# Gated linear attention and FFN on one core: the later units' state and score products in quarter tiles, joined into one row

## The chip, the cores and the metric

The kernel runs on one core of a Trainium2 chip. The metric is the device time of one execution in microseconds, as the median of several runs. Inside the core, TensorE multiplies matrices, VectorE, ScalarE and GpSimd work elementwise on what it leaves in PSUM, and SyncE's queue moves data by DMA. In the profile they are PE, DVE, ACT, POOL and SP; PEld is TensorE's loading of weights.

## The reference

Eight heads of four sequences, 768 tokens each, go through a linear attention whose state decays by a gate for each key dimension. Their outputs, 3072 tokens of 384, go through a two-layer FFN. q, k, v and alpha are float32, w_in and w_out are float64.

```python
for t in range(S):                       # S = 768; B, H, D = 4, 8, 48
    state = alpha[:, :, t, :, None] * state + np.einsum('bhd,bhe->bhde', k[:, :, t], v[:, :, t])
    y[:, :, t] = np.einsum('bhd,bhde->bhe', q[:, :, t], state)
x = y.transpose(0, 2, 1, 3).reshape(3072, 384)
h = x @ w_in                             # 384 x 2048
g = np.maximum(0.01 * h, h)
out = (g @ w_out).astype(np.float32)     # 2048 x 384
```

## The kernel before

**Attention.** The tokens are cut into chunks of 128. A unit u is one chunk of one sequence with all eight heads; there are 24, in order of the chunk and then of the sequence. Heads go in four pairs p, one head of a pair on partitions 0 to 47 (s = 0), the other on 64 to 111 (s = 1). For each unit, `scans` forms running products of alpha on VectorE (pc forward, rc backward), `scaled_q` and `scaled_k` transpose q and k and multiply them by these, and `scores` (L356) multiplies k by q for each head into two PSUM banks, which `mask_scores` copies and masks to sm (one bank on ScalarE and GpSimd, the other on VectorE, L364). `k_tokens` (L380) transposes k back to tokens. `outputs` then adds state times q (L395, for a pair at once, a block-diagonal 112x112 state) and values times masked scores (L401, two heads side by side in the columns), forms the new state's k v products (L412), and splits y into a high and a low part, ScalarE rounding it (L418) and VectorE subtracting (L419). `next_state` adds the products to the state (L436) and scales it by the decay on GpSimd (L373). In words used below: S is the scores, P state times q, V the values, K the k v products, t the transposes.

**FFN.** Three units make a block of 384 tokens; there are eight blocks. For each of 16 slices of 128 hidden columns, `ffn_in` makes one input product I: nine matmuls (three row groups of x, each as high x high, high x low, low x high) into a bank named ph (L493). ScalarE scales by 0.01 (L496), VectorE takes the maximum (L499), and the result is again split into gh (L501) and gl (L505). Three slices later `ffn_out` makes one output product O: nine matmuls into the block's three banks (L520). `gather` moves the spare rows of x into their places by DMA when a block's third unit is done.

**Order.** Units 0 to 8 come first (the head). Then blocks 0 and 1 run through the FFN while VectorE and ScalarE turn the float64 weights into high and low parts. From block 2 on, units 9 to 23, the later units, are woven in between the FFN's products: a generator yields slices of a unit's work, eight a unit (`SL`, `LEAD`), and the main loop takes as many as are due before each half item. A scheduler then fixes each engine's order by dependences; `tc.issue_after` pins an instruction behind another. PSUM has eight banks. Two rotate under ph; of six others, three hold a block's outputs (b) and three serve the attention (a). Tiles are given banks and SBUF as they are asked for, so a tile waits for whoever used its place before.

## Time and profile before

| | |
|---|---|
| runs | 531.2, 531.43, 532.03 us, median 531.43 us |
| profiled execution, span of the core | 530.9 us (page; what lies around the span isn't recorded for it) |
| granted TensorE clock, mean | 0.994 |
| TensorE busy | 518.5 us, 98% |
| VectorE busy | 379.0 us, 71% |
| ScalarE busy | 230.7 us, 43% |
| GpSimd busy | 62.6 us, 12% |

The page's lines give for each engine its busy time, its share of the span and the number of instructions. TensorE's rows count records: one float32 product is two records, so the scores' 8 products of a unit are 16. A row of a timeline has the start, the time in which the group was busy, engine, line, operation, output tile, input tiles, the tile of the array as rows*columns, the moving data and the count. The end of a matmul is modelled, so the time that a group takes is read from its start to the start of the next. A windows row has the window, its length, the busy time and count of each engine, the granted clock and the DMA share.

### The profile page before, as it was taken

The numbers are of one execution on the slowest core, as the hardware profiler recorded it, in microseconds if no ns is written. First come the engines' busy times: TensorE is split into PE (matmuls) and PEld (weight loads), VectorE is DVE, ScalarE is ACT, GpSimd is POOL, SyncE is SP. The second block draws the span as 40 slices with busy tenths as digits, with TensorE's granted clock in tenths as the row PEclk, the third lists the DMA queues.
The fourth block names the chain that finished last, engine by engine and source line by source line (L and its number), as shares of the span: only waits on it lengthen the run. The fifth ranks groups of instructions, "written<-read, shape, count | busy, mean of one in ns | idle before, by whom it ended". The sixth has DMA issues, their size and how long they took to land.

```text
span 530.9 us, 9962 instructions
## 1 busy us (share of the span) xinstructions
PE 518.5 (98%) x3778; PEld 500.0 (94%) x3778; DVE 379.0 (71%) x695; ACT 230.7 (43%) x489; POOL 62.6 (12%) x143
## 2 busy tenths in 40 slices
PE   8997999999999999999999999999999999999995
PEld 7886999999999999999999999999999999999995
DVE  6998899999999997777577586585786534333331
ACT  2764855555534444444334444345344444333331
POOL 4554500000000111100101101101010000000000
PEclk9998999999999999999999999999999999999998
DMA  9999975545726533552251431433201000101001
GB/s 144 168 175 170 229 172 133 131 122 141 170 45 184 127 84 81 102 134 49 60 111 30 112 83 44 92 74 86 54 15 25 31 16 1 23 1 44 1 0 51
DMA packets 92982, 46.64 MB, mean 88 GB/s; under 512 B 57856, under 2 KB 90112, under 8 KB 92928
## 3 DMA queue, kind: packets, MB, share of 16 engines
q1 hardware_dynamic: 92928, 45.93, 39.5%
q8 instruction: 32, 0.52, 0.4%
q14 instruction: 22, 0.18, 0.1%
HBM read 38.83 MB, written 4.72 MB: 82 GB/s over the span
## 4 chain that ended last, share of the span: by engine, by line
PE 87%; DVE 7%; DMA 4%; issue 1%; SPq 0%; DVEq 0%; ACT 0%
PE ph L493 35%; PE b L520 32%; PE a L356 4%; PE a L401 3%; PE a L520 3%; DMA small<-in_v_dram 3%; PE a L395 3%; PE a L412 2%; PE b L401 1%; PE a L380 1%; PE b L280 1%; DMA small<-in_alpha_dram 1%; DVE pw L262 1%; DVE gl L505 1%; DVE t L499 1%
## 5 line engine op out<-in xcount | busy, mean ns | idle before, releaser
L493 PE MATMUL ph<-large,w 128*128 128x384 f32 x1152 | 226.6, 338 | 0.5 <-DVE t L499 0.5
L493 PEld LDWEIGHTS ph<-large,w 128*128 128x128 f32 x1152 | 200.1, 188 | 2.8 <-DVE t L499 1.1
L520 PE MATMUL b<-w,gh 128*128 128x384 f32 x672 | 168.9, 340 | 0.0
L499 DVE TENSOR_TENSOR t<-ph,t 128x384 f32<-128x384 f32 x128 | 70.7, 553 | 79.1 <-ACT t L496 78.9
L520 PEld LDWEIGHTS b<-w,gh 128*128 128x128 f32 x672 | 119.4, 188 | 2.1 <-issue 0.4
L496 ACT ACTIVATE t<-ph 128x384 f32<-128x384 f32 x128 | 62.5, 489 | 128.2 <-PE ph L493 128.2
L501 ACT CAST gh<-t 128x384 fp32r<-128x384 f32 x128 | 65.7, 513 | 119.6 <-DVE t L499 119.6
L520 PE MATMUL b<-w,gl 128*128 128x384 f32 x336 | 107.4, 335 | 0.0
L505 DVE TENSOR_TENSOR gl<-t,gh 128x384 fp32r<-128x384 f32 x128 | 70.9, 554 | 34.3 <-ACT gh L501 34.2
L520 PEld LDWEIGHTS b<-w,gl 128*128 128x128 f32 x336 | 62.6, 188 | 0.0
L367 POOL TENSOR_SCALAR_AFFINE_SELECT sm<-sm 128x512 f32<-128x512 f32 x33 | 23.1, 712 | 207.8 <-ACT sm L366 207.8
L356 PEld LDWEIGHTS a<-qs,ks 48*128 48x128 f32 x312 | 24.1, 188 | 5.1 <-issue 4.2
L356 PE MATMUL a<-qs,ks 48*128 48x128 f32 x312 | 28.7, 285 | 0.0
L289 DVE STREAM_TRANSPOSE ks<-small 128x512 f32<-128x512 f32 x15 | 16.7, 1123 | 14.6 <-PE a L380 14.6
L324 POOL COPY pe<-pc 128x4 f32<-128x4 f32 x24 | 4.8, 202 | 163.7 <-DVE pc L314 163.7
L373 POOL TENSOR_TENSOR small<-us,pe 48x192 f32<-48x192 f32 x40 | 22.4, 560 | 1.5
L314 DVE TENSOR_TENSOR_SCAN pc<-e,small 128x128 f32<-128x128 f32 x60 | 20.4, 401 | 0.0
L366 ACT COPY sm<-a 128x512 f32<-128x512 f32 x24 | 14.0, 583 | 14.0 <-PE b L356 12.9
L520 PE MATMUL a<-w,gh 128*128 128x384 f32 x96 | 19.6, 337 | 0.0
L320 DVE TENSOR_TENSOR_SCAN rc<-e,small 128x511 f32<-128x511 f32 x15 | 19.1, 1276 | 0.2
L401 PE MATMUL a<-sm,small 128*48 128x128 f32 x256 | 17.7, 277 | 0.0
L254 ACT CAST w<-bits 128x768 fp32r<-128x768 f32 x16 | 13.4, 838 | 8.4 <-DVE bits L251 7.8
(92 smaller groups left out, 554.4 us busy)
## 6 DMA issues: line engine op xcount, KB each, us to landing
raw<-in_moe_w_out_dram SPq DMA_DIRECT2D x16, 384.0 KB, 3.8
small<-in_v_dram SPq DMA_DIRECT2D x24, 192.0 KB, 3.7
raw<-in_moe_w_in_dram SPq DMA_DIRECT2D x32, 144.0 KB, 4.0
out_dram<-o SPq DMA_DIRECT2D x24, 192.0 KB, 2.0
small<-in_alpha_dram SPq DMA_DIRECT2D x32, 96.0 KB, 2.3
small<-in_q_dram SPq DMA_DIRECT2D x30, 96.0 KB, 2.4
small<-in_k_dram SPq DMA_DIRECT2D x30, 96.0 KB, 2.2
small<-in_alpha_dram SPq DMA_DIRECT2D x30, 80.0 KB, 2.4
```

The source lines that it names most:

```text
L314: nc.vector.tensor_tensor_scan(pc[:, p, :], aT[:, p, :], ones.broadcast_to([P, C]), 1.0, ALU.mult, ALU.mult)
L320: nc.vector.tensor_tensor_scan(flat[2][:, NP * C - 2::-1], flat[0][:, NP * C - 1:0:-1], flat[1][:, NP * C - 2::-1], last, ALU.mult, ALU.add)
L356: nc.tensor.matmul(ss[s][:, p, :], ks[lo:lo + D, p, :], qs[lo:lo + D, p, :], start=True, stop=True)
L367: made["mask", u] = nc.gpsimd.affine_select(out=sm[s], in_=sm[s], compare_op=ALU.is_ge, fill=0.0, base=0, pattern=[[0, NP], [1, C]], chann ...
L373: nc.gpsimd.tensor_tensor(*scalings.pop(0))
L401: nc.tensor.matmul(y[lo:lo + m, p, :], V[:, c:c + m], masked[u][s][:, p, :], start=not tb and p == 0, stop=p == NP - 1, skip_group_check=True,
L493: nc.tensor.matmul(ph, w_in_of(f, wn, g), xt[:, g, :], start=n == 0, stop=n == 3 * NG - 1)
L496: put(ordered, "ACT", lambda: nc.scalar.mul(t, ph, 0.01))
L499: put(ordered, "DVE", lambda: nc.vector.tensor_tensor(t, ph, t, ALU.max))
L501: put(ordered, "ACT", lambda: nc.scalar.copy(gh, t))
L505: made["gl", i, f] = put(ordered, "DVE", lambda: nc.vector.tensor_tensor(gl, t, gh.bitcast(F32), ALU.subtract))
L520: product = nc.tensor.matmul(po[j], gt[:, js], w_out_of(f, wn), start=f == 0 and n == 0, stop=f == NF - 1 and n == 2)
```

## The change

**Scores.** For a later unit the 128 columns of weights are cut in two halves, M = HB = 64: 16 products, each on a quarter of the array (one half of the rows, one half of the columns), where there were 8 of half the array.

**State times q.** Four products of 112x112 become eight, one for each head, in the order that `heads` gives: q (0, 1), s (the head of the pair, the row half) and top (which pair, p = q + 2 top, the column half). A later unit uses 48 rows by 64 or 48 columns, a quarter; its two banks are one of the attention's, which also takes the k v products, and one of ph. An early unit uses 112 rows by 64 or 48 columns and one bank. `values` writes in the same places.

**One row.** `attention_later` replaces `attention` for units 9 to 23. It has seven slices a unit, and one of them issues past(u), scores(u+1), values(u) and products(u) with each instruction pinned behind the one before. I and O are pinned in the same line (`in_row`). The first scores wait until block 1's outputs are finished (`not (1 in pos and emitted == 3)`).

**x and tiles.** x now has heads 0 to 3 on the lower partitions and 4 to 7 on the upper; `runs`, which loads w_in's rows to match, changes in its first row and its strides, with as many DMAs of the same size. `split` copies a later unit's x in two halves, one for each bank. pe and us get fixed places (`ends_sb`, `sums_sb`), and pc and rc of later units one place each (`up`, `down`). The fallback `stepwise`, which these inputs do not reach, is adapted to the new places of x.

```diff
@@
     AHEAD = 3 * UPB
     LAG = 3
     SOON, EARLY = 2, 3
-    LEAD = 8
-    SL = 8 * UPB
+    LEAD = 7
+    SL = 7 * UPB
     kinds = ["a", "b"]
...
@@
-    runs = [(0, D, 0, 1, 2 * D), (D, GAP, 6 * D, NG, 1), (HB, D, D, 1, 2 * D), (BR, GAP, 7 * D, NG, 1)]
+    runs = [(0, D, 0, 1, D), (D, GAP, NG * D, NG, 1), (HB, D, NP * D, 1, D), (BR, GAP, (NP + NG) * D, NG, 1)]
     jobs = {}
@@
     def scans(u):
         aT = transposed(u, 0, "e", bufs=1)
-        pc = atp.tile([P, NP, C], F32, name="pc")
-        rc = atp.tile([P, NP, C], F32, name="rc")
-        pe = atp.tile([P, NP, 1], F32, name="pe", bufs=3)
+        pc, rc = (
+            atp.tile([P, NP, C], F32, name=name, bufs=2 if u < AHEAD else 1) for name in (("pc", "rc") if u < AHEAD else ("up", "down"))
+        )
+        pe = ends_sb[u % 3]
         for p in range(NP):
             nc.vector.tensor_tensor_scan(pc[:, p, :], aT[:, p, :], ones.broadcast_to([P, C]), 1.0, ALU.mult, ALU.mult)
         nc.vector.memset(every(aT, 0), 0.0)
@@
         pe, qs, ks = live[u]
         ss = [banks4(), banks4()]
+        M = C if u < AHEAD else HB
         for p in range(NP):
             for s, lo in ((0, 0), (1, HB)):
-                nc.tensor.matmul(ss[s][:, p, :], ks[lo:lo + D, p, :], qs[lo:lo + D, p, :], start=True, stop=True)
+                for t in range(0, C, M):
+                    yield ss[s][t:t + M, p, :], ks[lo:lo + D, p, t:t + M], qs[lo:lo + D, p, :], True, True
         live[u].append(ss)
     def mask_scores(u):
@@
             made["sm", u] = nc.scalar.copy(ktok.rearrange("t p d -> t (p d)"), kt[:, 0:NP * BR])
             live[u][2] = ktok
-    def outputs(u):
+    def heads():
+        for q in range(2):
+            for s, lo in ((0, 0), (1, HB)):
+                for top in range(2):
+                    yield q, s, lo, top, q + 2 * top, top * HB
+    ys = {}
+    def past(u):
         tb, b = units[u]
-        i, j = divmod(u, UPB)
+        qs, W = live[u][1], state[b].rearrange("r p n -> r (p n)")
+        if u < AHEAD:
+            y = banks4()
+            ys[u] = [y[:, s::2, :] for s in (0, 1)], y
+        else:
+            first = bank()
+            full = [first, ps_h.tile([P, 512], F32, name="ph")]
+            ys[u] = [t[:, 0:2 * C].rearrange("r (p n) -> r p n", p=2) for t in full], first[:, 2 * C:2 * C + NP * D]
+        if tb:
+            for q, s, lo, top, p, at in heads():
+                r = slice(0, BR) if u < AHEAD else slice(lo, lo + D)
+                c, m = p * BR + lo, D if top else HB
+                yield ys[u][0][s][at:at + m, q, :], W[r, c:c + m], qs[r, p, :], q == 0 and (s == 0 or u >= AHEAD), False
+    def values(u):
+        tb, b = units[u]
+        V = vals_sb[u % NV]
+        for q, s, lo, top, p, at in heads():
+            c = (2 * p + s) * D
+            m = D if top else HB
+            yield (
+                ys[u][0][s][at:at + m, q, :], V[:, c:c + m], masked[u][s][:, p, :],
+                not tb and q == 0 and s == 0, q == 1 and (s == 1 or u >= AHEAD),
+            )
+        del masked[u]
+    def products(u):
+        tb, b = units[u]
         pe, qs, ktok = live[u][:3]
-        V, W = vals_sb[u % NV], state[b]
-        at = i % 3 * (NG + 1)
-        y = banks4()
-        if tb:
-            for p in range(NP):
-                nc.tensor.matmul(
-                    y[0:BR, p, :], W[0:BR, p, :], qs[0:BR, p, :], start=p == 0, stop=False, skip_group_check=True
-                )
-        for p in range(NP):
-            for s, lo, m in ((0, 0, D if tb else HB), (1, HB, D)):
-                c = (2 * p + s) * D
-                nc.tensor.matmul(
-                    y[lo:lo + m, p, :], V[:, c:c + m], masked[u][s][:, p, :],
-                    start=not tb and p == 0, stop=p == NP - 1, skip_group_check=True,
-                )
-        del masked[u]
+        V = vals_sb[u % NV]
         kv = None
         if tb < NC - 1:
-            kv = bank()[:, 0:NP * D].rearrange("d (p e) -> d p e", p=NP)
+            kv = ys[u][1] if u >= AHEAD else bank()[:, 0:NP * D]
+            kv = kv.rearrange("d (p e) -> d p e", p=NP)
             for p in range(NP):
                 for s, lo, m in ((0, 0, HB), (1, HB, D)):
                     h = 2 * p + s
-                    made["kv", u] = nc.tensor.matmul(
-                        kv[lo:lo + m, p, :], ktok[:, p, lo:lo + m], V[:, h * D:(h + 1) * D], start=True, stop=True
-                    )
+                    yield kv[lo:lo + m, p, :], ktok[:, p, lo:lo + m], V[:, h * D:(h + 1) * D], True, True
         load_values(u + NV)
         live[u] = pe, kv
+    row = []
+    def multiply(groups, row=None):
+        for group in groups:
+            for out, weights, moving, start, stop in group:
+                with tc.issue_after(row[-1].ins) if row else nullcontext():
+                    made["product",] = nc.tensor.matmul(out, weights, moving, start=start, stop=stop, skip_group_check=True)
+                if row is not None:
+                    row[:] = [made["product",]]
+    def split(u):
+        i, j = divmod(u, UPB)
+        at = i % 3 * (NG + 1)
+        pair, y = ys.pop(u)
         xh, xl = (x_sb[0:BR, at:at + NP, n, j * C:(j + 1) * C] for n in (0, 1))
-        made["xh", u] = nc.scalar.copy(xh, y[0:BR])
-        made["x", u] = nc.vector.tensor_tensor(xl, y[0:BR], xh.bitcast(F32), ALU.subtract)
+        for h, l, t in [(xh, xl, y)] if u < AHEAD else [(xh[:, s::2, :], xl[:, s::2, :], pair[s]) for s in (1, 0)]:
+            made["xh", u] = nc.scalar.copy(h, t[0:BR])
+            made["x", u] = nc.vector.tensor_tensor(l, t[0:BR], h.bitcast(F32), ALU.subtract)
     def next_state(u):
         tb, b = units[u]
...
@@
                 scans(u + 1)
                 yield
             if old:
-                scores(u)
+                multiply([scores(u)])
                 yield
                 mask_scores(u)
                 yield
@@
                 scaled_k(u + 1)
                 yield
             if old:
-                outputs(u)
+                multiply([past(u), values(u), products(u)])
+                split(u)
                 yield
                 next_state(u)
                 if u % UPB == UPB - 1:
                     gather(u // UPB)
                     ready.add(u // UPB)
                 yield
+    def attention_later(first, last):
+        for u in range(first - 1, last):
+            new, old = u + 1 < last, u >= first
+            if old:
+                k_tokens(u)
+                yield
+            if new:
+                scans(u + 1)
+                yield
+                scaled_q(u + 1)
+                yield
+                scaled_k(u + 1)
+                sum_up(u + 1)
+                yield
+            groups = [past(u)] if old else []
+            if new:
+                groups.append(scores(u + 1))
+            if old:
+                groups += [values(u), products(u)]
+            multiply(groups, row)
+            if old:
+                split(u)
+            yield
+            if new:
+                mask_scores(u + 1)
+                yield
+            if old:
+                next_state(u)
+                if u % UPB == UPB - 1:
+                    gather(u // UPB)
+                    ready.add(u // UPB)
+                yield
+    def in_row():
+        return tc.issue_after(row[-1].ins) if row else nullcontext()
     def ffn_in(i, f, steps=None):
@@
         xh, xl = xs[i]
         ph = ps_h.tile([P, 512], F32, name="ph")[:, 0:TB]
         n = 0
-        for g in range(NG):
-            for wn, xt in ((HIGH, xh), (HIGH, xl), (LOW, xh)):
-                nc.tensor.matmul(ph, w_in_of(f, wn, g), xt[:, g, :], start=n == 0, stop=n == 3 * NG - 1)
-                n += 1
+        with in_row():
+            for g in range(NG):
+                for wn, xt in ((HIGH, xh), (HIGH, xl), (LOW, xh)):
+                    product = nc.tensor.matmul(ph, w_in_of(f, wn, g), xt[:, g, :], start=n == 0, stop=n == 3 * NG - 1)
+                    n += 1
+        if row:
+            row[:] = [product]
         t = ffp.tile([P, TB], F32, name="t")
         put(ordered, "ACT", lambda: nc.scalar.mul(t, ph, 0.01))
         for step in first:
@@
         for j in range(UPB):
             js = slice(j * C, (j + 1) * C)
-            with behind("last"):
+            with behind("last"), in_row():
                 for n, (gt, wn) in enumerate(((gh, HIGH), (gh, LOW), (gl, HIGH))):
                     product = nc.tensor.matmul(
                         po[j], gt[:, js], w_out_of(f, wn), start=f == 0 and n == 0, stop=f == NF - 1 and n == 2
                     )
             if i == NB - 1 and f == NF - 1:
                 made["last",] = product
+        if row:
+            row[:] = [product]
         if f == NF - 1:
             finish(i)
@@
             i, f, slices, _ = items[n]
             if f == 0:
                 if i == 2:
-                    st, held = attention(AHEAD, NU), HELD
+                    st, held = attention_later(AHEAD, NU), HELD
                 while i not in ready:
                     next(st)
                 emitted, due = 0, 0.0
@@
                 gs[n] = ffn_in(i, f)
         for half in range(2):
             due += slices / 2
-            while emitted < due:
+            while emitted < due and not (1 in pos and emitted == 3):
                 with behind("gl", *held.pop(0)) if held else nullcontext():
                     next(st, None)
                 emitted += 1
...
```

What follows are rows of each engine's order, a run of like instructions to a row: line, operation, output and input tiles, shape, count. First TensorE before, through one later unit in the middle of the stage: L356 is S, L380 t, L395 P, L401 V, L412 K, L493 and L520 the FFN's I and O.

```order
L493 MATMUL ph<-large,w_942 128x384 x9
...
L356 MATMUL a<-qs,ks 128x128 x8
L493 MATMUL ph<-large,w_1017 128x384 x9
...
L380 MATMUL a<-small,ks 128x112 x4
...
L493 MATMUL ph<-large,w_1181 128x384 x9
L395 MATMUL a<-qs,small 112x128 x4
L401 MATMUL a<-sm,small 48x128 x8
L412 MATMUL a<-small,ktok 64x48
L412 MATMUL a<-small,ktok 48x48
...
L520 MATMUL b<-w_1017,gh 128x384 x2
```

The scores stand two items of the FFN ahead of the transposes, and these two ahead of the rest. TensorE after the change, at such a place; the attention's products all have the line of `multiply`, L452, and are told apart by their inputs (qs,small is P, qs,ks S, sm,small V, small,ktok K), while L578 is I and L607 O:

```order
L578 MATMUL ph<-large,w_1622 128x384 x9
L452 MATMUL a<-qs,small 64x128
L452 MATMUL a<-qs,small 48x128
L452 MATMUL ph<-qs,small 64x128
L452 MATMUL ph<-qs,small 48x128
...
L452 MATMUL a<-qs,ks 64x128 x16
L452 MATMUL a<-sm,small 64x128
L452 MATMUL a<-sm,small 48x128
L452 MATMUL ph<-sm,small 64x128
L452 MATMUL ph<-sm,small 48x128
...
L452 MATMUL a<-small,ktok 64x48
...
L607 MATMUL b<-w_1433,gh 128x384 x2
```

P of one unit, S of the next, V and K now stand in one run between an I and an O. P and V write to a bank of the attention and a bank ph in turn.

The second place is the start of the later stage on TensorE, from the last output product of block 1 (to a) on. Before:

```order
L520 MATMUL a<-w_1805,gl 128x384 x3
L520 MATMUL b<-w_667,gh 128x384 x4
...
L493 MATMUL ph<-large,w_1017 128x384 x9
L520 MATMUL b<-w_801,gh 128x384 x5
L356 MATMUL a<-qs,ks 128x128 x8
L380 MATMUL a<-small,ks 128x112 x4
L493 MATMUL ph<-large,w_1035 128x384 x9
```

And after:

```order
L607 MATMUL a<-w_1811,gl 128x384 x3
L452 MATMUL a<-qs,ks 64x128 x16
L578 MATMUL ph<-large,w_1023 128x384 x9
L607 MATMUL b<-w_663,gh 128x384 x2
...
L578 MATMUL ph<-large,w_1041 128x384 x4
L385 MATMUL a<-small,ks 128x112 x4
L578 MATMUL ph<-large,w_1041 128x384 x5
...
L578 MATMUL ph<-large,w_1109 128x384 x9
L452 MATMUL a<-qs,small 64x128
```

S of unit 9 has moved ahead of the first output product of block 2 (b), the transposes stand inside an I, and the first joined row comes three input products behind that S. On VectorE at the same place, up to the max (L586) of the I in which the transposes stand:

```order
L317 SCALAR_TENSOR_TENSOR up<-e,small 128x128
L369 TENSOR_TENSOR sm<-a,small 128x512
L317 SCALAR_TENSOR_TENSOR up<-e,small 128x128 x3
L318 MEMSET e 128x32
L319 RECIPROCAL small<-up 128x32
L586 TENSOR_TENSOR t<-ph,t 128x384
L323 SCALAR_TENSOR_TENSOR down<-e,small 128x511
L592 TENSOR_TENSOR gl<-t,gh 128x384
L291 STREAM_TRANSPOSE e<-small 128x4x4x32
L291 STREAM_TRANSPOSE ks<-small 128x4x4x32
L350 TENSOR_TENSOR ks<-ks,down 128x512
L586 TENSOR_TENSOR t<-ph,t 128x384
```

Here L317 and L323 are the scans (up, down), L291 the transposes of alpha, q and k, L350 the product of k, L369 the mask, L586 and L592 the FFN's max and low part. The transposes and products of unit 10's k now stand ahead of that max.

More of the change, by code (lines that the diff above doesn't have):

```diff
@@ L426, in next_state @@
         W = state[b]
-        us = atp.tile([P, NP, D], F32, name="us" if tb else f"us{b}", bufs=2 if tb else 1)
+        us = sums_sb[u % 2] if tb else atp.tile([P, NP, D], F32, name=f"us{b}", bufs=1)
         if tb == 0:
@@ L633, in stepwise @@
         L, V = [by_token(loads_sb[i][0]) for i in range(3)], vals_sb[0]
-        def place(h, e):
-            return (h // 2) * HB + e if h < 2 * NG else e % NG * HB + D + e // NG
         E4 = 4
@@ L655, in stepwise @@
                 aT, qT, kT = T
-                yt = [gps.tile([P, NG, HB], F32, name=f"yt{s}") for s in (0, 1)]
+                yt = [gps.tile([P, NP, D], F32, name=f"yt{s}") for s in (0, 1)]
                 for p in range(NP):
@@ L683, in stepwise @@
                 y = gp.tile([P, DM], F32, name="y", bufs=1)
-                for s in (0, 1):
-                    nc.vector.tensor_copy(y.rearrange("t (g s r) -> t g s r", g=NG, s=2)[:, :, s, :], yt[s])
+                to = y.rearrange("t (g top r) -> t g top r", g=NG, top=2)
+                for top in (0, 1):
+                    for slot in range(NP):
+                        made_by = yt[slot % 2][:, 2 * top + slot // 2, :]
+                        if slot < NG:
+                            nc.vector.tensor_copy(to[:, slot, top, 0:D], made_by)
+                        else:
+                            nc.vector.tensor_copy(
+                                to[:, :, top, D:].rearrange("t g r -> t r g"), made_by.rearrange("t (r g) -> t r g", g=NG)
+                            )
                 xT = gps.tile([P, NG, C], F32, name="gT")
```

7 lines of the change are left out of this document (4 added, 3 removed).

## Prediction

> **What bounds the kernel now.** I read the page's totals and its chain first, then windows by stage, then TensorE's timeline of one unit of the attention.
>
> ```profile
> span 530.9 us, 9962 instructions
> PE 518.5 (98%) x3778; PEld 500.0 (94%) x3778; DVE 379.0 (71%) x695; ACT 230.7 (43%) x489; POOL 62.6 (12%) x143
> PE 87%; DVE 7%; DMA 4%; issue 1%; SPq 0%; DVEq 0%; ACT 0%
> PE ph L493 35%; PE b L520 32%; PE a L356 4%; PE a L401 3%; PE a L520 3%; DMA small<-in_v_dram 3%; PE a L395 3%; PE a L412 2%; PE b L401 1%; PE a L380 1%; PE b L280 1%; DMA small<-in_alpha_dram 1%; DVE pw L262 1%; DVE gl L505 1%; DVE t L499 1%
> ```
>
> TensorE is busy 98% of the span and 87% of the chain. In the chain's shares by line 67% is the FFN (L493 and L520 to tile b), which the change leaves alone, and 4 + 3 + 3 + 2% the attention's products (L356, L401, L395, L412), which it rewrites.
>
> ```profile
> core 0: us, PE busy (x) PEld busy (x) DVE busy (x) ACT busy (x) POOL busy (x), PEclk, DMA share, GB/s
> 160.00:240.00 80.00, 79.53 (x605) 76.50 (x603) 66.44 (x123) 34.12 (x78) 10.60 (x25) 1.00 0.48 117
> ```
>
> Where the later units begin, TensorE is busy 79.53 of 80 us at full clock (column PEclk), and VectorE 66.44/80 = 83%. So a microsecond taken from a later unit's products is one off the end, as long as VectorE keeps up. Busy time counts modelled ends, so I cost groups from start to start, on the timeline:
>
> ```profile
> 261.99 0.55 PE L380 MATMUL a<-small,ks 112*128 112x112 f32 x4
> 262.30 0.59 PE L520 MATMUL b<-w,gh 128*128 128x384 f32 x2
> ...
> 263.97 1.72 PE L493 MATMUL ph<-large,w 128*128 128x384 f32 x9
> ...
> 267.10 1.72 PE L493 MATMUL ph<-large,w 128*128 128x384 f32 x9
> 268.66 1.04 PE L395 MATMUL a<-qs,small 112*112 112x128 f32 x8
> 269.63 1.08 PE L401 MATMUL a<-sm,small 128*48 128x128 f32 x16
> 270.54 0.61 PE L412 MATMUL a<-small,ktok 128*64 128x48 f32 x16
> 271.08 0.62 PE L520 MATMUL b<-w,gh 128*128 128x384 f32 x2
> ...
> 272.77 1.72 PE L493 MATMUL ph<-large,w 128*128 128x384 f32 x9
> 274.32 0.52 PE L520 MATMUL b<-w,gh 128*128 128x384 f32 x2
> ...
> 275.89 1.72 PE L493 MATMUL ph<-large,w 128*128 128x384 f32 x9
> 277.55 1.16 PE L356 MATMUL a<-qs,ks 48*128 48x128 f32 x16
> 278.64 0.61 PE L520 MATMUL b<-w,gh 128*128 128x384 f32 x2
> ...
> 280.33 0.85 PE L493 MATMUL ph<-large,w 128*128 128x384 f32 x4
> ```
>
> Undisturbed, an input product I takes 267.10 to 268.66 = 1.56 us, an output product O 274.32 to 275.89 = 1.57. The records come two to each product of the attention.
>
> - Scores S: 277.55 to 278.64 = 1.09, and they disturb their neighbours: the I ahead takes 1.66 (+0.10), the O behind 1.69 (+0.12). Together 1.31.
> - State times q, P: 0.97 (8 records, one after the other).
> - Values V: 0.91 for 16 records, 0.114 a pair. State products K: 0.54, and the O behind takes 1.69 (+0.12).
> - Transposes t: 0.31, and the O behind 1.67 (+0.10).
>
> A later unit costs 1.31 + 0.97 + 0.91 + 0.54 + 0.12 = **3.85 us**, besides t (0.41, kept).
>
> **The change part by part.** *Quarter tiles.* P becomes 8 products of 48 rows by 64 or 48 columns, S 16 of 48 rows by 64. If the four quarters run abreast, that is 2 rounds of q for P, each of two records: 4 rounds; S has 32 records, 8 rounds. No row shows four abreast. V shows two column tiles abreast at 0.114 a pair, though both use all rows; S shows two row tiles abreast at 1.09/8 = 0.136, with its own start and end in it. A quarter still has 128 columns to move, so 0.11 is the lower end; two pairs one after the other, 0.23, the upper. I take 0.112, the rate of V's pairs without the group's ends. Then P + S = 12 x 0.112 = 1.34.
>
> [...]
>
> *One row.* Around S the array changes its form twice: 0.10 on the I ahead, 0.12 on the O behind, and inside S itself 1.09 - 8 x 0.112 = 0.19. That is 0.41, about 0.2 each way. In the joined row, I to quarters costs 0.20 once, quarters to V is bounded by nothing and that 0.41; I take 0.10, near what P has now beyond the rate of V's pairs (0.97 - 8 x 0.112 = 0.07). The way out behind K stays 0.12. New row: 0.20 + 1.34 + 0.10 + 0.91 + 0.54 + 0.12 = **3.21**, 0.64 less.
>
> *Over the 15 later units* there are 14 joined rows; S of unit 9 stands alone, before the first (0.2 + 0.90 + 0.2 = 1.30), and the last row has no S (0.20 + 0.45 + 0.10 + 0.91 + 0.12 = 1.78). Leaving out K, which is unchanged: 15 x 3.31 = 49.65 before, 14 x 2.67 + 1.30 + 1.78 = 40.46 after: **-9.2**. Transposes: five times three of them stand ahead of an I and one behind, and once all four in an I's middle; each is one more change of form, 0.1 each: **+0.6**.
>
> *Fixed buffers, names of tiles, the split in two halves.* No arithmetic is added. Two copies of half size on ScalarE and VectorE cost two starts more a unit; VectorE's idle share (17% and more) hides them. Without that cover a start of some 0.1 x 15 would be 1.5. The early units' P takes 16 records by 64 columns, at V's rate 0.91 against 0.97. I put that, the other order of w_in rows (as many pieces, of the same size) and the wait for v there at nothing, within 1 us either way.
>
> *Waits at the start of the later stage.* The array's order is now pinned, and VectorE comes out of the weight conversion with a backlog, as its timeline shows:
>
> ```profile
> 167.27 1.38 DVE L314 TENSOR_TENSOR_SCAN pc<-e,small 128x128 f32<-128x128 f32 x4
> 169.03 0.35 DVE L316 RECIPROCAL small<-pc 128x32 f32<-128x32 f32 x1
> 169.26 0.66 DVE L339 TENSOR_TENSOR qs<-qs,pc 128x512 f32<-128x512 f32 x1
> 169.81 1.30 DVE L320 TENSOR_TENSOR_SCAN rc<-e,small 128x511 f32<-128x511 f32 x1
> 171.00 0.56 DVE L505 TENSOR_TENSOR gl<-t,gh 128x384 fp32r<-128x384 f32 x1
> 171.44 0.58 DVE L499 TENSOR_TENSOR t<-ph,t 128x384 f32<-128x384 f32 x1
> 171.91 0.71 DVE L347 TENSOR_TENSOR ks<-ks,rc 128x512 f32<-128x512 f32 x1
> 172.51 1.14 DVE L289 STREAM_TRANSPOSE e<-small 128x512 f32<-128x512 f32 x1
> 173.47 0.56 DVE L505 TENSOR_TENSOR gl<-t,gh 128x384 fp32r<-128x384 f32 x1
> 175.55 0.68 DVE L364 TENSOR_TENSOR sm<-a,small 128x512 f32<-128x512 f32 x1
> 176.15 1.10 DVE L289 STREAM_TRANSPOSE ks<-small 128x512 f32<-128x512 f32 x1
> 177.10 1.42 DVE L314 TENSOR_TENSOR_SCAN pc<-e,small 128x128 f32<-128x128 f32 x4
> ```
>
> And TensorE's timeline there:
>
> ```profile
> 168.42 0.85 PE L520 MATMUL b<-w,gh 128*128 128x384 f32 x4
> 183.65 1.88 PE L356 MATMUL a<-qs,ks 48*128 48x128 f32 x16
> 185.46 0.62 PE L520 MATMUL b<-w,gh 128*128 128x384 f32 x2
> ```
>
> First: at 168.42 the array now takes S (1.19 with its way in) and an I (1.66) and reaches block 2's first O at 171.27. The bank of that O was an I's, and is free when the max begun at 171.44 ends, at 172.02: **0.75**. Second: the scores of the first joined row use a bank that waits for the max of the I three before it. VectorE's queue up to there, from 172.51: transpose 0.96, gl 0.44, four scans and a max 1.76 (167.27 to 169.03), mask 0.60, reciprocal 0.23, long scan 1.19, gl 0.44, two transposes 0.96 and 0.95, the k product 0.60 and the max 0.58, to 181.22. The array gets there at 172.02 + O 1.57 + I with t in its middle 2.07 + O 1.57 + I 1.56 + 0.20 + P 0.45 = 179.44: **1.8**. Everything of the row and the FFN is queued behind it. Of today's stalls one goes: S at 183.65 takes 1.81 instead of 1.09, **-0.7**.
>
> Sum: -9.2 + 0.6 + 0.75 + 1.8 - 0.7 = -6.8 us. The profiled span is 530.9, and the median of the runs 531.43, so 0.5 lies around the span; the same 0.5 stays. 531.4 - 6.8 = **524.6 us**.
>
> **The rivals.** *Two abreast only* (slower). If quarters that share rows or columns follow one another, 12 rounds take 0.224 instead of 0.112: 1.34 more a row, 15 x 1.34 = 20.1, 544.7. For it: no row shows four streams, and records of K come at 0.54/16 = 34 ns, above the 28 ns that four abreast need. Against it: K's have fewer columns and were not short of weights, and V and S each show one half of what is needed. It decides from 6.8/15/12 = 0.038 a round, at 0.15; between 0.15 and 0.23 the kernel is slower.
>
> *New waits in every row.* P's second bank was an I's, two groups before: O 1.57, I 1.56 and 0.3 leave 3.4 us for ScalarE's and VectorE's passes of that I. At 83% VectorE may be late by more. 0.2 to 0.35 in each of 15 rows is 3 to 5 us: 527.6 to 529.8. Against it: by the durations above the max stands ahead of the row's work in VectorE's queue, with a microsecond to spare. [...]
>
> *No wait at the start.* If VectorE's order there lets the two maxima through, 2.5 less: 522.1; with a free change from quarters to V also 1.5 less: 520.6.
>
> *Nothing gained.* Were the chain through VectorE or the transfers, the freed time would come back as idle time: 531.4. The windows of TensorE without idle time speak against it.
>
> **How the numbers follow.** Forecast, 523 to 527: 0.55. New waits, 527 to 530: 0.17. No start wait, 520 to 523: 0.12. Within 0.2% (1.06 us, about what a measurement of this kernel can tell from no change), from gains eaten by rounds of 0.14 to 0.16: 0.06. Slower, by rounds above that: 0.10. Faster is 0.84. The range 520.5 to 530.0 leaves out the last two and little else.
>
> **What would show it.** P and S in one row of 48 records starting about 28 ns apart, 1.3 to 1.4 us together; about 56 ns would be the first rival. A unit's products 3.2 instead of 3.85 in the windows from 190 us on. Two gaps on TensorE between 171 and 182 of 0.75 and 1.8, released by VectorE's max. The head's end, where the first output product starts, within 1 us of before. Wrong would be idle time of TensorE inside later rows, released by VectorE's max or by the gathers of x.

## The result, and the profile after

| | before | after |
|---|---|---|
| runs, us | 531.16 to 532.03 (4), median 531.32 | 525.64 to 526.41 (4), median 526.08 |
| ratio of the times | | 0.990, 95% interval 0.988 to 0.991 |
| profiled execution: span, us | 530.9 | 523.9 |
| TensorE busy, us | 518.5 | 508.2 |

The kernel became 5.2 us faster, 1.0%; 6.8 had been forecast (524.6, range 520.5 to 530.0). The page after the change:

```profile
span 523.9 us, 10785 instructions
PE 508.2 (97%) x4178; PEld 487.1 (93%) x4178; DVE 385.1 (73%) x710; ACT 233.5 (45%) x504; POOL 69.6 (13%) x143
PE 63%; DVE 20%; DMA 8%; issue 4%; SPq 2%; ACT 1%; POOL 0%; DVEq 0%; ACTq 0%
```

TensorE's share of the chain (what ended last, followed back) fell from 87% to 63%, VectorE's rose from 7% to 20%. Followed back, the chain now leaves TensorE at a wait at 191 us and runs on through VectorE and transfers of the time before; so the shares show that there are waits, not how long they are. The windows by stage (the same columns as before):

```profile
160.00:240.00 80.00, 75.33 (x704) 71.03 (x703) 68.24 (x129) 34.75 (x87) 13.04 (x24) 1.00 0.44 111
240.00:320.00 80.00, 80.00 (x716) 77.90 (x715) 59.07 (x112) 34.62 (x79) 9.43 (x20) 1.00 0.33 79
```

At the start of the later stage TensorE is idle 4.7 of 80 us, where it had been 0.5; from 240 on it is busy but for some tenths. Now TensorE's timeline of one joined row, between an output and an input product:

```profile
290.34 0.51 PE L607 MATMUL b<-w,gh 128*128 128x384 f32 x2
...
291.99 0.32 PE L452 MATMUL a<-qs,small 48*64 48x128 f32 x2
292.00 0.32 PE L452 MATMUL ph<-qs,small 48*64 48x128 f32 x2
292.14 0.28 PE L452 MATMUL a<-qs,small 48*48 48x128 f32 x2
...
292.47 1.05 PE L452 MATMUL a<-qs,ks 48*64 48x128 f32 x32
293.46 0.43 PE L452 MATMUL a<-sm,small 128*64 128x128 f32 x4
...
294.37 0.62 PE L452 MATMUL a<-small,ktok 128*48 128x48 f32 x16
294.92 1.85 PE L578 MATMUL ph<-large,w 128*128 128x384 f32 x9
296.62 0.51 PE L607 MATMUL b<-w,gh 128*128 128x384 f32 x2
```

From start to start: 0.08 extra on the O ahead (1.65), P 0.48, S 0.99, V 0.91, K 0.55, 0.14 extra on the I behind (1.70). Together 3.15 us; 3.21 had been forecast, 3.85 is the cost before. Four quarters start within 0.02 us, and S's 32 records take 8 rounds of 0.11.

TensorE's waits in the later stage of the same trace, with what ended them in brackets:

```profile
169.61 0.62 PE L607 MATMUL b<-w,gh 128*128 128x384 f32 x2 [0.66 <-DVE t L586]
179.65 1.09 PE L452 MATMUL a<-qs,ks 48*64 48x128 f32 x28 [2.30 <-DVE t L586]
191.07 1.86 PE L578 MATMUL ph<-large,w 128*128 128x384 f32 x9 [0.42 <-DVE t L586]
213.44 0.32 PE L452 MATMUL ph<-qs,small 48*64 48x128 f32 x2 [0.74 <-DVE t L586]
340.17 1.80 PE L578 MATMUL ph<-large,w 128*128 128x384 f32 x9 [0.28 <-DVE small L481]
```

The first two are the forecast ones, with the same releaser, VectorE's maximum. Three more, and a short one at 224, were not foreseen. A bracket counts from the modelled end of the matmul ahead; from start to start the first costs 0.82, the second 2.5, and the later ones 0.58, 0.92, 0.14 and 0.45, that is 2.1 us.

Where the rest of the difference lies is read from the first output product and the last one of the three traces: before as shown above, before in another execution (the first experiment below), and after.

```profile
66.78 0.51 PE L520 MATMUL b<-w,gh 128*128 128x384 f32 x2
525.03 0.34 PE L520 MATMUL b<-w,gl 128*128 128x384 f32 x1
```

```profile
65.00 0.51 PE L520 MATMUL b<-w,gh 128*128 128x384 f32 x2
523.21 0.34 PE L520 MATMUL b<-w,gl 128*128 128x384 f32 x1
```

```profile
64.15 0.51 PE L607 MATMUL b<-w,gh 128*128 128x384 f32 x2
518.16 0.34 PE L607 MATMUL b<-w,gl 128*128 128x384 f32 x1
```

From first to last it is 458.25, 458.21 and 454.01 us: beyond the head the change brought 4.2, not 6.8. The heads differ by up to 2.6, of which 1.8 is between two executions of one kernel.

### The profile page after: what moved, and what is told of

Same layout as the page of the kernel before. It is cut to its first block, busy times and chain, and to the rows that moved or that the text cites. A ratio compares the mean times of both kernels' runs of the same rounds, so it can differ in the third digit from the quotient of the medians.

```text
span 523.9 us, 10785 instructions
## 1 busy us (share of the span) xinstructions
PE 508.2 (97%) x4178; PEld 487.1 (93%) x4178; DVE 385.1 (73%) x710; ACT 233.5 (45%) x504; POOL 69.6 (13%) x143
## 4 chain that ended last, share of the span: by engine, by line
PE 63%; DVE 20%; DMA 8%; issue 4%; SPq 2%; ACT 1%; POOL 0%; DVEq 0%; ACTq 0%
PE b L607 26%; PE ph L578 26%; PE a L452 6%; DVE pw L264 3%; DVE gl L592 2%; DMA raw<-in_moe_w_in_dram 2%; DVE bits L262 2%; DVE bits L253 2%; DVE t L586 2%; DMA small<-in_alpha_dram 2%; DMA small<-in_v_dram 2%; PE ph L452 1%; DVE pw L260 1%; DVE bits L250 1%; DMA raw<-in_moe_w_out_dram 1%
## 5 line engine op out<-in xcount | busy, mean ns | idle before, releaser
L578 PE MATMUL ph<-large,w 128*128 128x384 f32 x1152 | 226.6, 337 | 1.3 <-DVE t L586 1.0
L578 PEld LDWEIGHTS ph<-large,w 128*128 128x128 f32 x1152 | 199.8, 188 | 5.1 <-DVE t L586 2.2
L607 PE MATMUL b<-w,gh 128*128 128x384 f32 x672 | 167.2, 336 | 0.7 <-DVE t L586 0.7
L607 PEld LDWEIGHTS b<-w,gh 128*128 128x128 f32 x672 | 120.1, 188 | 1.8 <-DVE t L586 1.0
L586 DVE TENSOR_TENSOR t<-ph,t 128x384 f32<-128x384 f32 x128 | 70.5, 550 | 66.4 <-ACT t L583 66.0
L607 PE MATMUL b<-w,gl 128*128 128x384 f32 x336 | 107.7, 335 | 0.0
L592 DVE TENSOR_TENSOR gl<-t,gh 128x384 fp32r<-128x384 f32 x128 | 70.7, 553 | 41.9 <-ACT gh L588 41.9
L607 PEld LDWEIGHTS b<-w,gl 128*128 128x128 f32 x336 | 62.6, 188 | 0.0
L372 POOL TENSOR_SCALAR_AFFINE_SELECT sm<-sm 128x512 f32<-128x512 f32 x33 | 29.1, 893 | 203.3 <-ACT sm L371 125.6
L452 PE MATMUL a<-qs,ks 48*64 48x128 f32 (+1 forms) x552 | 27.1, 272 | 2.3 <-DVE t L586 2.3
L317 DVE TENSOR_TENSOR_SCAN up<-e,small 128x128 f32<-128x128 f32 x60 | 21.1, 411 | 8.5 <-ACT up L335 8.5
L452 PEld LDWEIGHTS a<-qs,ks 48*64 48x64 f32 (+1 forms) x552 | 22.9, 140 | 3.8 <-DVE t L586 2.5
L607 PE MATMUL a<-w,gh 128*128 128x384 f32 x96 | 19.5, 334 | 0.0
L323 DVE TENSOR_TENSOR_SCAN down<-e,small 128x511 f32<-128x511 f32 x15 | 19.2, 1280 | 0.4
L335 ACT ACTIVATE up<-up 128x512 f32<-128x512 f32 x15 | 9.5, 633 | 20.9 <-POOL small L327 16.9
L378 POOL TENSOR_TENSOR small<-small 48x192 f32<-48x192 f32 x32 | 18.3, 572 | 1.2
L327 POOL COPY small<-up 128x4 f32<-128x4 f32 x15 | 3.3, 221 | 104.4 <-DVE up L317 103.7
L291 DVE STREAM_TRANSPOSE qs<-small 128x512 f32<-128x512 f32 x15 | 17.0, 1132 | 0.0
```

The lines of the kernel that those rows point to most:

```text
L291: nc.vector.transpose(t.rearrange("r p (j t) -> r p t j", t=T4), src.rearrange("r p (t d) -> r p t d", t=T4)[:, :, :, 0:32],)
L317: nc.vector.tensor_tensor_scan(pc[:, p, :], aT[:, p, :], ones.broadcast_to([P, C]), 1.0, ALU.mult, ALU.mult)
L323: nc.vector.tensor_tensor_scan(flat[2][:, NP * C - 2::-1], flat[0][:, NP * C - 1:0:-1], flat[1][:, NP * C - 2::-1], last, ALU.mult, ALU.add)
L372: made["mask", u] = nc.gpsimd.affine_select(out=sm[s], in_=sm[s], compare_op=ALU.is_ge, fill=0.0, base=0, pattern=[[0, NP], [1, C]], chann ...
L378: nc.gpsimd.tensor_tensor(*scalings.pop(0))
L452: made["product",] = nc.tensor.matmul(out, weights, moving, start=start, stop=stop, skip_group_check=True)
```

## The experiments

All but the first are edits of the changed kernel. Each was timed against the kernel before on the same chip; the ratio of the two, with its interval, is given in parentheses where it decides. The chip was not the same one for all experiments, so between two experiments the ratios are what to compare, and a difference within the intervals is settled by the traces at most. Only edited lines are shown.

**The kernel before, once more.** No edit.

> The kernel before, unchanged, to see the spread of its head and its time around the span. If the earlier start of the output products (64.15 us after the change, 66.78 before, behind a wait of 2.8 us for v) belongs to the change, the profile taken here has its first output product at 66.5 to 67, the wait for v, and the span is 530.5 to 531.5, about 0.5 below the time. If it was chance of one execution in a head that waits for transfers, the first output product here may lie at 64 to 65, and the spans near 529.5, 1.7 below the time as in the changed kernel (525.64 with a span of 523.9).

Measured: 531.13 us (ratio 1.000, 0.999 to 1.002); the profiled execution took 530.85 with a span of 529.1, and in all 12 runs time less span was 1.7 to 1.8. The first output product stood at 65.00. So chance: if 1.7 us lay around its span too, and not 0.5, the execution from which the prediction was made took about 1.3 us more than the median. What made its head longer stands in the two traces: first the shown execution, then this one.

```profile
49.98 0.42 PE L401 MATMUL b<-sm,small 128*48 128x128 f32 x1 [2.79 <-DMA small<-in_v_dram]
49.75:53.16 3.41, 3.18 (x34) 2.85 (x36) 2.29 (x6) 0.20 (x1) 0.19 (x1) 0.50 0.82 121
```

```profile
48.33 0.28 PE L401 MATMUL b<-sm,small 128*48 128x128 f32 x1 [1.24 <-DMA small<-in_v_dram]
```

TensorE waited 2.79 us for v there and 1.24 here, and behind the longer wait its granted clock was half (0.50) from 49.75 to 53.16 us; here it was full (1.00) throughout the head. In the profiled executions of the changed kernel and its eleven variants below the first output product stands between 64.15 and 64.97, so some tenths of a microsecond of the head may still be the change's; that is open.

**Past in column tiles.** P of later units in the form of the early ones.

```diff
-            full = [first, ps_h.tile([P, 512], F32, name="ph")]
-            ys[u] = [t[:, 0:2 * C].rearrange("r (p n) -> r p n", p=2) for t in full], first[:, 2 * C:2 * C + NP * D]
+            y = ps_h.tile([P, 512], F32, name="ph").rearrange("r (p n) -> r p n", p=NP)
+            ys[u] = [y[:, s::2, :] for s in (0, 1)], first[:, 2 * C:2 * C + NP * D]
...
-                r = slice(0, BR) if u < AHEAD else slice(lo, lo + D)
+                r = slice(0, BR)
...
```

The start and stop flags are set for the one bank to match.

> The changed kernel with state times q of the later units in column tiles of all 112 rows, as the early units have it, into one bank ph. Theory, quarters run four abreast: these 16 records run two abreast, 8 rounds of 0.109 instead of 4, 0.87 instead of 0.48 and one more change of form of 0.1 to 0.2, so 0.45 to 0.6 more in each of 15 rows, 7 to 9 us: 532.5 to 535. Rival, the joined row is what gains and the quarters nothing: 526 to 527.

Measured: 532.07 us (ratio 1.002, 1.001 to 1.003). The row, on TensorE's timeline:

```profile
271.20 1.09 PE L452 MATMUL ph<-qs,small 112*64 112x128 f32 x16
272.22 1.10 PE L452 MATMUL a<-qs,ks 48*64 48x128 f32 x32
273.25 1.09 PE L452 MATMUL ph<-sm,small 128*64 128x128 f32 x16
```

P takes 1.02 instead of 0.48, S 1.03 instead of 0.99: 0.58 more, in 15 rows 8.7, less some 2 of waits that this order doesn't have. Of P's 0.54 some 0.44 are the four rounds more of 0.11; the rest goes with one more change of form. Quarters four abreast are worth more than the whole gain; the rival of two abreast is out, as the four starts within 0.02 us above show as well.

**Scores apart.** S in a slice of its own, behind the row by an item; a unit then has eight slices.

```diff
-    LEAD = 7
-    SL = 7 * UPB
+    LEAD = 8
+    SL = 8 * UPB
...
-            groups = [past(u)] if old else []
-            if new:
-                groups.append(scores(u + 1))
-            if old:
-                groups += [values(u), products(u)]
+            groups = [past(u), values(u), products(u)] if old else []
             multiply(groups, row)
             if old:
                 split(u)
-            yield
+                yield
             if new:
+                multiply([scores(u + 1)], row)
+                yield
                 mask_scores(u + 1)
```

> The changed kernel with the scores in a slice of their own (8 a unit, LEAD 8), an output or input product behind the row; still in quarters. Theory: S alone has its own way in and out, 1.3 us as before the change instead of 0.98 + 0.05 inside the row, so 0.35 to 0.45 more in each of 14 rows, 5 to 6 us, less 1 to 2.5 of waits that may go with the other order: 529 to 531. Rival, joining gains nothing and the waits rule: 523.5 to 525.

Measured: 529.13 us (0.996, 0.994 to 0.997). S alone, between an input and an output product:

```profile
272.45 1.73 PE L576 MATMUL ph<-large,w 128*128 128x384 f32 x9
274.10 1.10 PE L452 MATMUL a<-qs,ks 48*64 48x128 f32 x32
275.14 0.62 PE L605 MATMUL b<-w,gh 128*128 128x384 f32 x2
```

From start to start the row without S is 2.28, S alone 1.24 with its disturbance of both neighbours: 3.52 against 3.15, 5.2 us in 14 rows. The time rose by 3.1; TensorE's waits in this trace are some 1.4 shorter in all (from start to start), and the rest was not traced. Joining gains about what was claimed for it.

**Scores last.** S behind K in the same row.

```diff
-            groups = [past(u)] if old else []
+            groups = [past(u), values(u), products(u)] if old else []
             if new:
                 groups.append(scores(u + 1))
-            if old:
-                groups += [values(u), products(u)]
```

> The changed kernel with the scores behind the state products in the same row: past, values, products, scores. The same products, one more change of the array's form from K to S and a dearer way out. Theory, changes of form cost: K to S 0.2 and S to the output product 0.2 in place of S to V 0.1 and K to the output product 0.12: 0.2 to 0.3 more for each of 14 rows, 3 to 4 us, so 529 to 530. Rival, forms cost nothing and only the four quarters abreast count: 525.7 to 526.5.

Measured: 524.08 us (0.987, 0.985 to 0.989): faster than the change, against both expectations.

```profile
268.73 0.32 PE L452 MATMUL a<-qs,small 48*64 48x128 f32 x2
...
269.32 0.43 PE L452 MATMUL a<-sm,small 128*64 128x128 f32 x4
...
270.24 0.62 PE L452 MATMUL a<-small,ktok 128*48 128x48 f32 x16
270.79 1.10 PE L452 MATMUL a<-qs,ks 48*64 48x128 f32 x32
271.82 0.62 PE L605 MATMUL b<-w,gh 128*128 128x384 f32 x2
```

P to V 0.59, V 0.92, K 0.55, S 1.03, and 0.10 on either neighbour: 3.19, only 0.04 above the row of the change. With one change of form more the row is 0.04 longer, not 0.2 to 0.3. What was gained came from the waits. V and K stand ahead of the scores that wait, so that one is 0.71, not 2.30; and on VectorE the split of x stands ahead of the next scans in every row, so the later waits are down to one, of 0.73.

**Where the later waits come from.** VectorE's timeline of the changed kernel behind the row at 196 us shows a wait for ScalarE (L335, the sum pass), and ScalarE's own shows one for GpSimd (L327, the copy of the last column of up):

```profile
200.81 0.41 DVE L464 TENSOR_TENSOR large<-ph,large 112x256 fp32r<-112x256 f32 x1
202.28 1.37 DVE L317 TENSOR_TENSOR_SCAN up<-e,small 128x128 f32<-128x128 f32 x4 [1.06 <-ACT up L335]
203.57 0.40 DVE L464 TENSOR_TENSOR large<-a,large 112x256 fp32r<-112x256 f32 x1
```

```profile
201.52 0.63 ACT L335 ACTIVATE up<-up 128x512 f32<-128x512 f32 x1 [2.32 <-POOL small L327]
```

The scans stand ahead of half of the split, and they overwrite up, which has one place. Three edits tried this.

*Ends on ScalarE.*

```diff
-        nc.gpsimd.tensor_copy(pe, pc[:, :, C - 1:C])
+        (nc.gpsimd.tensor_copy if u < AHEAD else nc.scalar.copy)(pe, pc[:, :, C - 1:C])
```

> The changed kernel, but for later units ScalarE copies the last column of up to its fixed place instead of GpSimd. Orders of TensorE and VectorE stay as they are. Theory: the waits of TensorE at 190, 212, 224 and 340 us (0.58, 0.92, 0.12 and 0.45, together 2.1) come from up having one place: the next unit's scans wait for ScalarE's sum pass, that for GpSimd's copy, and that stands behind a mask and two scalings; with the copy on ScalarE they go, VectorE's idle time ahead of the scans falls from 8.5 us to below 2, and the time to 523.9 to 524.7. Rival, VectorE's load as such: the same waits, 525.7 to 526.4.

Measured: 526.02 us (0.990, 0.988 to 0.992), as the change; VectorE's idle time ahead of the scans 8.2. GpSimd still stood in the chain: ScalarE's copy waited 13.7 us for GpSimd's scalings (L378), which read the place that the copy writes. The waits at 190 and 224 were gone, 0.52 at 216 and 0.4 at 342 were left. But TensorE's granted clock was half (0.50) in this trace from 179.68 to 186.50 us, which puts TensorE off by itself (more on this under the clock, below). Inconclusive.

*Four places for the ends.*

```diff
-        *[(NP, 1)] * 3, *[(NP, D)] * 2
+        *[(NP, 1)] * 4, *[(NP, D)] * 2
...
-        pe = ends_sb[u % 3]
+        pe = ends_sb[u % 4]
```

> The changed kernel with four fixed places for the last column of up (ends_sb) instead of three; nothing else is edited. The copy on ScalarE alone did not take the waits at 215 and 342 us away: it stood behind GpSimd's scaling of the state, for the place it writes was still read by that scaling, one unit late since the masks moved behind the row. Theory: with a fourth place GpSimd may copy ahead of the mask and the scalings, ScalarE's sum pass and VectorE's scans follow at once, and the waits at 190, 212, 224 and 340 (2.1 us) go, the two at 169 and 177 stay: 523.7 to 524.5. Rival, VectorE's load or the one place of up itself: VectorE still idles ahead of its scans, 525.5 to 526.4.

> Scores behind the state products in the row, and four places for the ends: the two edits together. The run with the scores last had 1.07 us at 198 and 0.8 at 178 left besides the 0.75 at 169. Theory: the one at 198 goes, 523.0; if the two edits act on the same wait, 524.0 as with the scores last alone.

Measured: 541.69 us (1.018, 1.016 to 1.021), and 535.74 with the scores last. Both expectations failed. With one dependence less, the scheduler wrote other orders on ScalarE, GpSimd and VectorE, and new waits came, up to

```profile
308.12 0.72 PE L607 MATMUL b<-w,gh 128*128 128x384 f32 x2 [2.31 <-ACT o L621]
```

where a block's first output product waits for ScalarE to copy out the block before. So this says nothing on up; it says how far the orders can move by an edit of 16 bytes a partition. Which of the new positions costs most was not tried.

*Scans behind the split.*

```diff
-        for p in range(NP):
-            nc.vector.tensor_tensor_scan(pc[:, p, :], aT[:, p, :], ones.broadcast_to([P, C]), 1.0, ALU.mult, ALU.mult)
+        with behind("x", u - 3) if u > AHEAD else nullcontext():
+            for p in range(NP):
+                nc.vector.tensor_tensor_scan(pc[:, p, :], aT[:, p, :], ones.broadcast_to([P, C]), 1.0, ALU.mult, ALU.mult)
```

> The changed kernel with the scans of a later unit pinned on VectorE behind the splitting of x that is due before them (unit u behind unit u - 3). The orders of TensorE, ScalarE and GpSimd stay as they are; on VectorE the scans move behind the split (and the sum of the state) in four places, after the rows at 180, 196, 212 and 332 us, and nowhere else. Theory: TensorE's waits at 190, 212, 224 and 340 us come from these four: VectorE stood there 0.8 to 1.7 us before scans whose one place, up, was still being read, with the split and the FFN's maximum queued behind them. Then all four go, the two at 169 and 177 stay, and the time falls by 2: 523.8 to 524.5. Rival, VectorE's load over the unit: the waits come back behind other operations, 525.5 to 526.4.

Measured: 526.02 us (0.990, 0.988 to 0.992), as the change. In its trace VectorE's idle time ahead of the scans is 3.8 instead of 8.5 us, and the waits at 190, 224 and 340 are gone, 1.2 us from start to start. The one at 212 stays (0.66 at 215): the maximum that ends it comes only 0.1 earlier against the array's row, so that is VectorE's load. At 340 the pin did what was expected: the sums that TensorE waited for come 1.0 us earlier against the array. At 190 this trace can't tell. First the maximum that ended that wait, in the changed kernel, then the same one here:

```profile
190.46 0.56 DVE L586 TENSOR_TENSOR t<-ph,t 128x384 f32<-128x384 f32 x1
```

```profile
190.44 0.56 DVE L587 TENSOR_TENSOR t<-ph,t 128x384 f32<-128x384 f32 x1
```

It is no earlier; TensorE came 2.85 us later, because its clock had been halved. So the wait is gone, but the pin isn't shown to have removed it.

**The clock behind a long wait.** The scores that wait, in the trace of the scans behind the split, with its windows around them; then two windows of the changed kernel, whose row stands above (1.09 for the same 28 records):

```profile
179.54 1.97 PE L453 MATMUL a<-qs,ks 48*64 48x128 f32 x28 [2.32 <-DVE t L587]
175.82:179.23 3.41, 1.40 (x24) 0.91 (x22) 3.31 (x6) 0.68 (x3) 0.00 (x0) 1.00 0.21 58
179.23:186.06 6.83, 6.52 (x66) 6.10 (x67) 5.60 (x11) 3.58 (x10) 0.81 (x1) 0.50 0.60 147
186.06:189.47 3.41, 3.41 (x22) 3.41 (x21) 3.25 (x9) 0.49 (x1) 1.17 (x1) 1.00 0.14 30
```

```profile
175.31:178.73 3.42, 2.04 (x28) 1.55 (x26) 3.31 (x5) 0.84 (x3) 0.00 (x0) 1.00 0.13 34
178.73:182.14 3.41, 2.49 (x60) 2.26 (x61) 2.69 (x5) 2.27 (x6) 0.00 (x0) 1.00 0.80 192
```

The column ahead of the last two is the granted clock: 0.50 from 179.23 to 186.06 us in the one, 1.00 throughout in the other, after waits of the same length. S, V, K and the O behind them took 9.9 us instead of 6.9, so in this trace the clock cost 3.0 us, more than the waits that are gone. The medians don't settle what the pin is worth: the mean clock of a run is 0.994 to 1.000 in the changed kernel's four and 0.992 to 0.999 in these six, but the one run at 0.999 took 526.4 us, so the clock is not all of it.

What told the two apart can be read from the traces. Half the clock lasts 6.83 us here, full clock then 337.92 until the next change at 523.98: 2 and 99 steps of 3.413 us. In the changed kernel the clock changes at 523.48, behind the last product; counted back from there in such steps, a boundary falls at 178.73 and parts the wait of 2.30 us into 1.38 (3.42 less 2.04 busy) and 0.92. In the other trace a boundary falls at 179.23, and 2.01 us of the wait lie in one step. In the later stages of all the traces here, the eight steps at full clock in which TensorE was idle for 1.58 us or more were followed by half the clock, the six with 1.19 to 1.56 were not; at the very end of the runs some with up to 1.86 were not either. No run was made to move a wait against the steps, so this is how 14 traces agree, not a test.

**The wait of the first row.** First by moving the row:

```diff
-    LEAD = 7
+    LEAD = 3
```

> The changed kernel with LEAD = 3 instead of 7: block 2 takes 24 slices over its 16 items instead of 28, and unit 9's row stands one output and one input product later, 3.1 us. Theory, the wait of 2.3 us of the first joined row is VectorE's backlog of one moment: it falls below 0.5, the 0.7 of the first output product stays; the later waits are of another kind and stay, some at other places: 523.5 to 524.5. Rival, the row waits by its place in the rotation of banks wherever it stands: 2 us there again, 525.5 to 526.5.

Measured: 530.04 us (0.998, 0.996 to 1.000). The row's wait fell only to 1.38, at P's second bank, and all of unit 11 came too late:

```profile
226.43 3.10 PE L578 MATMUL ph<-large,w 128*128 128x384 f32 x9 [4.69 <-DMA large<-large]
```

Block 3's first input product waited 4.7 us for the gather of its x, and its nine matmuls ran at half the clock (0.50 from 225.84 to 229.25 us). LEAD pays for that transfer.

Then two places for up, in the kernel with the scores last:

```diff
-            atp.tile([P, NP, C], F32, name=name, bufs=2 if u < AHEAD else 1) for name in (("pc", "rc") if u < AHEAD else ("up", "down"))
+            atp.tile([P, NP, C], F32, name=name, bufs=1 if name == "down" else 2) for name in (("pc", "rc") if u < AHEAD else ("up", "down"))
```

> The kernel with the scores last in the row, and two places for up instead of one; TensorE's order is that of the run with the scores last. There VectorE has the split ahead of the scans at every row already. Theory: then one place costs nothing any more, and two give 523.8 to 524.5, as with one. Rival, the one place costs by itself: 522.5 to 523.3, with the wait of 0.73 at 199 gone.

Measured: 527.39 us (0.993, 0.991 to 0.994), 3.3 more than with one place; both theories missed. From start to start the first row's scores now wait 1.8 us instead of 0.9. Behind that wait the clock was half (0.50) from 182.64 to 186.05 us, and the O and the I that follow took 2.51 and 2.45 us instead of 1.67 and 1.56. So in the traces, which differ by 2.7 us from the end of block 1 to the last output product, 1.0 is the wait and 1.7 the clock. VectorE's timeline there:

```profile
178.40 1.29 DVE L317 TENSOR_TENSOR_SCAN up<-e,small 128x128 f32<-128x128 f32 x4
...
180.21 0.54 DVE L584 TENSOR_TENSOR t<-ph,t 128x384 f32<-128x384 f32 x1
```

With room, VectorE runs further ahead: the next unit's scans now stand in front of the maximum (L584) that the scores wait for.

Last, the work that runs ahead, pinned later at that one place:

```diff
-        aT = transposed(u, 0, "e", bufs=1)
+        with behind(*("gl", 2, 5)) if u == AHEAD + 3 else nullcontext():
+            aT = transposed(u, 0, "e", bufs=1)
...
-        kT = transposed(u, 2, "ks")
+        with behind(*("gl", 2, 5)) if u == AHEAD + 2 else nullcontext():
+            kT = transposed(u, 2, "ks")
```

> The changed kernel with two steps of VectorE pinned a little later at the start of the stage: unit 11's transpose and product of k, and unit 12's transpose of alpha, stand behind the low part of block 2's sixth input product instead of ahead of the maximum that the first joined row's scores wait for. Every other order stays, but for two lines on ScalarE. Theory: VectorE runs ahead there with work that nobody needs yet, 2.5 us of it; without it the wait of 2.3 us at 177 falls below 0.4, no clock below full speed follows it, and the time is 523.3 to 524.3. Rival, VectorE's backlog is a sum of work and only moves: the wait at 177 goes, but the input products at 183 to 192 wait 1.5 to 2.5 us longer, 525.5 to 526.3.

Measured: 524.54 us (0.988, 0.986 to 0.990), 1.5 less than the change by the medians; the two intervals overlap, but the trace agrees, with 350.5 us instead of 352.4 from the end of block 1 to the last output product. The wait at 177 is gone; that at 190 grew from 0.42 to 0.98, that at 212 from 0.74 to 0.89, and 0.28 at 338 stays. So the theory holds for most of it, the rival for some 0.7: with the first wait gone, the array is ahead of VectorE at the next ones. The runs' mean clock is 0.998 to 1.000.

> The same two pins in the kernel with the scores last in the row, which had 0.71 at 179 and 0.73 at 199. Theory: the one at 179 goes, 523.0 to 523.7. Rival, the backlog only moves: 524.0 to 524.6.

Measured: 522.16 us (0.985, 0.982 to 0.987), the fastest of all by the median, under both expectations: the wait at 199 went too (one of its five runs took 524.72, at a mean clock of 0.991). One is left on TensorE in the later stage:

```profile
169.55 0.62 PE L607 MATMUL b<-w,gh 128*128 128x384 f32 x2 [0.68 <-DVE t L586]
```

## Why the prediction was right, and where it was off

- **Quarter tiles** (12 rounds of 0.112): right, four abreast at 0.11 a round; two quarters of one row half start 0.01 us apart, all four within 0.02. A pair of column tiles (V, 0.114 a pair) had shown one half of this and a pair of row tiles (S, 0.136 a pair) the other.
- **One row** (3.21): measured 3.15, and 3.52 with S apart. What was mis-sized is the way into the quarters: 0.12 (0.08 on the O ahead and 0.04 in P beyond four rounds) where 0.20 had been put.
- **First wait** (0.75): 0.82 from start to start. **Second wait** (1.8): 2.5. VectorE's queue up to that maximum was 0.8 longer than the sum of its durations from the trace before: 0.6 in four scans and the maximum among them, 0.2 in a transpose of k.
- **"Fixed buffers, names of tiles, the split in two halves" at nothing:** this is the step that failed. The average idle time of VectorE (17%) did not hide them (a half-size copy took 0.42 and 0.41 us on VectorE where the whole had taken 0.68, and 0.37 on ScalarE instead of 0.59, so a second start was some 0.15 on either, not 0.1), because the order of VectorE's instructions is fixed: at 340 scans that wait for their one place keep the split and the sums behind them, and after the start VectorE's backlog delays its maxima until 213 us. That made four more waits, 2.1 us. Pinning the scans behind the split took the one at 340 away; that at 212 stayed, and at 190 the halved clock hides what the pin did. With the split ahead of the scans in every row one of 0.73 was left, and with some of VectorE's early work pinned later as well none: so order and backlog together are the cause, and how the 2.1 us divide between them is open. The rival of new waits had the right kind and the right place (P's second bank, an I's bank), in four rows, not all.
- **The base** ("the same 0.5 stays", the head "within 1 us either way"): 1.7 lie around each span, not 0.5, and the shown execution had a head 1.8 us longer than another one of the same kernel. That did no harm to the forecast, which was taken off the median of the runs. But between the profiled execution of the first experiment and that of the change, of 5.2 us 4.2 lie between the first and the last output product, 0.85 in the head and 0.2 at the end; so 1.0 of the gain was not forecast, and that the time came as near to 524.6 as it did is to that extent luck.
- **The sum**, beyond the head: -6.8 forecast; -0.8 for the rows being 0.06 shorter, +0.1 for the first wait, +0.7 for the second and +2.1 for the new ones make -4.7; measured is -4.2. Of the 0.5 left, 0.2 lie ahead of the later stage (101.7 us from the first output product to the end of block 1, against 101.4 and 101.5 before). The rest was not traced to its end. The extra 0.6 for split transposes was too much: in the trace three ahead of an I and one behind cost 0.45 with what they add to their neighbours, four together 0.42. Against that, what follows a wait takes longer (the I behind the one at 190 1.70 instead of 1.56).

## What to carry over

Small products of the same form are worth packing and joining: here joining saved 0.37 us a row and packing some 0.5. When that makes the bound engine faster, look next at the queue of the engine that empties its banks, instruction by instruction and at the stage's start, since an average of idle time doesn't say when an engine whose order is fixed gets to the one instruction that others wait for. More room made this kernel slower: a fourth place 541.69 us instead of 526.08, a second buffer 527.39 instead of 524.08. With the second buffer the trace shows why: what runs ahead stands in front of what is waited for, and the longer wait (1.8 us instead of 0.9) had half the clock behind it (0.50 for 3.41 us).

## What was not expected of the hardware

Two things. Waits of TensorE of 2.3 us were followed by half the clock (0.50 for 6.83 us) in some executions and by full clock in others; which of the two followed agrees, in the later stages of the 14 traces, with how much of the wait lay in one step of 3.413 us (1.58 us or more, or 1.56 or less), and no run tested it. So one wait cost 3.0 us beyond its length in one trace, and hid another wait. And time less span was 1.6 to 1.8 us in every run of every kernel, so two spans may be compared without it, while one execution of a head that waits for transfers lay 1.8 us from the next.
